# Seven block products in place of eight for the first product of a second mixture of experts

## The chip, the cores and the metric

The kernel runs on one core of one Trainium2 chip. The metric is the device time in microseconds (us) of one execution. Three runs of the kernel before took 2059.77, 2060.48 and 2062.86 us; their median is 2060.48 us. One more execution was profiled.

The engines are named as in the profile: PE is TensorE (matrix products; PEld its weight loads), DVE is VectorE, ACT is ScalarE, POOL is GpSimd, SP is SyncE, which here only issues DMA transfers.

## The reference

Three stages follow one another on 2304 tokens of width 512:

```
x   = attention(q, k, v)        # 4 x 8 heads, 576 positions, windows of 32, plain or dilated by 4
h   = x @ w_in                  # 512 -> 2048        (first mixture, rational activation)
x   = (P(h) / Q(h)) @ w_out     # 2048 -> 512, P and Q polynomials of third and second degree
Pr  = exp(x @ w_gate - max); 8 times: divide by row sums, by column sums, times N / 8
out = sum over e of Pr[:, e] * (relu(x @ w1[e]) @ w2[e])     # 8 experts, 512 -> 1024 -> 512
```

Inputs and outputs are float32. The products of the two mixtures are made of pieces: each operand is scaled by a power of two and split into a high and a low part in float16 (in the first mixture's second product, without scaling, in a reduced float32), and hi*hi + hi*lo + lo*hi are summed, so each product costs three matrix instructions.

## The kernel before, in words

**First mixture.** It runs in 96 steps (`NS1`): six blocks of 384 tokens (`NB`, `TB`) times sixteen blocks of 128 features. A step makes 12 instructions of the first product (`rat_l1`, L574 to L576), the rational function on ACT, DVE and POOL (`rat_a`, `rat_b`, `rat_c`, L589 to L612), and three steps later 12 instructions of the second product (`rat_l2`, L626 to L628). Attention of later batches is woven between the steps. When a block of tokens is done, `x2_evac` takes it out of PSUM, `x2_absmax` finds its scale (L655), and `x2_split` makes the float16 pieces of the block on ACT and DVE (L151, L154), which stay in SBUF.

**Second mixture.** It runs in 288 slots (`NS2`): eight experts, nine pairs of token tiles of 128 (`PAIRS`), four groups of hidden features (`NP`), each with 128 features of the lower and 128 of the upper half. In a slot `moe_l1` makes the first product directly: 2 halves x 4 blocks of the contraction x 3 instructions = 24 instructions of 256 columns (L826). `moe_a` applies the relu on ACT (L843), forms four sums and differences of blocks on POOL (L845), and splits seven blocks into hi and lo on ACT and DVE (L848, L849). Two slots later (`LAG2`) `moe_l2` makes the second product as seven block products instead of eight (`PRODS`): 21 instructions of 256 columns (L867 to L869). After the fourth group `y_evac` puts the seven products together on DVE (L905) and adds the gated result to a sum in SBUF (L913), which is written out once, during the last expert (L915).

**Weights.** For each expert, eight pieces of 512 KB (`raw_load`, on SP's queue) are loaded twice: once to find the scale (`raw_absmax`, L759), once to be split (`raw_part`, L786 on ACT and L789 on DVE). Pieces of `w2` also get four differences on POOL (`raw_diff`, L796). Times of this work are written out by hand with `at(...)`; what is pinned by `pin` stays behind the same engine's work on the current group. Within that, a scheduler of the framework fixes the order of each engine's instructions when the program is built, and each engine then runs its own list in that order.

**PSUM.** Two sets of four banks: `bank` for products that are taken out at once, `long` for sums that live over many instructions. The second product of the second mixture uses all four `long` banks.

## Time and profile before

| what | value |
|---|---|
| median of three runs | 2060.48 us |
| span of the profiled execution | 2059.4 us |
| PE busy | 1975.8 us, 96% of the span |
| DVE, ACT, POOL busy | 1360.0, 1033.1, 876.1 us |
| chain that ended last | PE 70%, DVE 8%; L826 35%, L867 to L869 10% each |
| moved by DMA | 112.32 MB |

The profiled execution took 2059.4 us from its first to its last instruction; that is 1.1 us less than the median of the runs. Busy time is the union of an engine's instructions. Matrix instructions overlap in the records, so their pitch (start to start) tells more than their duration. A group of the page names the source line, engine, operation and tiles, the count, the busy time, the mean of one, and the idle time before them with what ended it.

### The profile page before, as it was taken

To read this page: it belongs to the slowest core of one execution; us is meant where nothing else is said; L and a number is where in the kernel's file an instruction comes from. 1 tells how busy PE (TensorE), PEld (TensorE's weight loads), DVE (VectorE), ACT (ScalarE), POOL (GpSimd) and SP (SyncE) were. 2 spreads that over 40 slices of the span, in tenths; PEclk is the share of its full clock that TensorE was granted. 3 is DMA by queue.
4 is the path that set the end of the run, shared out by engine and by line. 5 is a ranking of instruction groups with operands and counts; after the bars stand their busy time and mean duration, and the time that the engine had idled before them with its cause. 6 is when DMAs were issued, how large, how long until landed. Compare 5 with 4: busy or idle time off the path is not lost.

```text
span 2059.4 us, 42175 instructions
## 1 busy us (share of the span) xinstructions
PE 1975.8 (96%) x16764; PEld 1707.6 (83%) x16764; DVE 1360.0 (66%) x2441; ACT 1033.1 (50%) x1981; POOL 876.1 (43%) x1471
## 2 busy tenths in 40 slices
PE   7588999999999999999999999999999999999998
PEld 6466767776778888888888888888888888888887
DVE  5898899889997654655665564565556546556344
ACT  5777888776775344344434434433443443334332
POOL 1232233222244355445545545454454545446333
PEclk7789999999999999999999999999999999999999
DMA  6642220113111111300211130021112102110000
GB/s 169 165 139 77 61 73 13 35 28 98 32 32 52 52 42 32 93 22 22 78 52 37 35 90 27 27 83 42 32 42 83 32 22 88 37 32 12 32 32 32
DMA packets 171637, 112.32 MB, mean 55 GB/s; under 512 B 74160, under 2 KB 156080, under 8 KB 171440
## 3 DMA queue, kind: packets, MB, share of 16 engines
q1 hardware_dynamic: 171440, 109.64, 18.3%
q8 instruction: 131, 2.15, 0.4%
q14 instruction: 66, 0.54, 0.1%
HBM read 104.88 MB, written 4.72 MB: 53 GB/s over the span
## 4 chain that ended last, share of the span: by engine, by line
PE 70%; DVE 8%; ACT 2%; POOL 1%; issue 1%; DMA 1%; SPq 0%; DVEq 0%; POOLq 0%; ACTq 0%
PE h2ps L826 35%; PE yps L867 10%; PE yps L868 10%; PE yps L869 10%; POOL ht L845 1%; DVE slab_a L603 1%; DVE slab_q L592 1%; DVE slab_q L602 1%; DVE slab_t L604 1%; PE o1ps L626 1%; DVE slab_t L594 1%; PE o1ps L627 1%; PE o1ps L628 1%; DMA wraw<-in_moe_w_dram 1%; DVE slab_t L593 1%
## 5 line engine op out<-in xcount | busy, mean ns | idle before, releaser
L845 POOL TENSOR_TENSOR ht<-ht 128x128 f32<-128x128 f32 x1152 | 607.9, 548 | 719.4 <-ACT ht L843 697.1
L826 PE MATMUL h2ps<-xs,w1t 128*128 128x256 f16 x6912 | 803.8, 273 | 0.0
L826 PEld LDWEIGHTS <-w1t 128*128 128x128 f16 x6912 | 675.6, 98 | 78.9 <-issue 1.1
L849 DVE TENSOR_TENSOR hs<-ht,hs 128x896 f16<-128x896 f32 x288 | 331.8, 1153 | 557.1 <-ACT hs L848 557.1
L848 ACT ACTIVATE hs<-ht 128x896 f16<-128x896 f32 x288 | 273.2, 950 | 623.7 <-POOL ht L845 623.6
L867 PE MATMUL yps<-w2t,hs 128*128 128x256 f16 x2016 | 548.1, 273 | 0.3 <-DVE ys L905 0.3
L868 PE MATMUL yps<-w2t,hs 128*128 128x256 f16 x2016 | 548.1, 273 | 0.0
L869 PE MATMUL yps<-w2t,hs 128*128 128x256 f16 x2016 | 545.6, 273 | 0.0
L843 ACT ACTIVATE ht<-h2ps 128x512 f32<-128x512 f32 x288 | 170.2, 592 | 213.9 <-PE h2ps L826 212.1
L868 PEld LDWEIGHTS <-hs 128*128 128x128 f16 x2016 | 197.2, 98 | 23.8 <-issue 0.5
L869 PEld LDWEIGHTS <-hs 128*128 128x128 f16 x2016 | 197.3, 98 | 23.0
L867 PEld LDWEIGHTS <-hs 128*128 128x128 f16 x2016 | 197.3, 98 | 22.6
L612 POOL TENSOR_TENSOR slab_g<-slab_t,slab_g 128x384 fp32r<-128x384 f32 x96 | 107.0, 1117 | 240.7 <-ACT slab_g L611 176.4
L905 DVE TENSOR_TENSOR ys<-yps,ys 128x256 f32<-128x256 f32 x468 | 168.3, 418 | 53.0 <-ACT ys L900 45.1
L627 PE MATMUL o1ps<-slab_g,wo_hi 128*128 128x384 f32 x384 | 139.7, 364 | 2.4 <-POOL slab_g L612 2.1
L628 PE MATMUL o1ps<-slab_g,wo_lo 128*128 128x384 f32 x384 | 132.6, 345 | 0.0
L626 PE MATMUL o1ps<-slab_g,wo_hi 128*128 128x384 f32 x384 | 105.0, 374 | 9.6 <-ACT slab_g L611 8.7
L574 PE MATMUL h1ps<-x,wi 128*128 128x384 f16 x256 | 85.7, 335 | 9.9 <-DMA qks<-in_q_dram 3.5
L913 DVE SCALAR_TENSOR_TENSOR acc<-ys,pwt,acc 128x512 f32<-128x512 f32 x112 | 90.8, 811 | 0.0
L575 PE MATMUL h1ps<-x,wi 128*128 128x384 f16 x256 | 85.3, 333 | 0.0
L576 PE MATMUL h1ps<-x,wi 128*128 128x384 f16 x256 | 85.1, 332 | 0.0
L626 PEld LDWEIGHTS o1ps<-slab_g,wo_hi 128*128 128x128 f32 x384 | 68.6, 194 | 17.0 <-ACT slab_g L611 12.5
(163 smaller groups left out, 2456.1 us busy)
## 6 DMA issues: line engine op xcount, KB each, us to landing
wraw<-in_moe_w_dram SPq DMA_DIRECT2D x192, 256.0 KB
wraw<-in_moe_w_dram SPq DMA_DIRECT2D x128, 128.0 KB
wst<-in_moe_w_in_dram SPq DMA_DIRECT2D x16, 512.0 KB
xs<-in_v_dram SPq DMA_DIRECT2D x6, 768.0 KB
xs<-in_moe_w_out_dram SPq DMA_DIRECT2D x9, 512.0 KB
out_dram<-acc SPq DMA_DIRECT2D x16, 256.0 KB
wost<-in_moe_w_out_dram SPq DMA_DIRECT2D x7, 512.0 KB
...
```

Of the source, the lines that this page charges most:

```text
L626: nc.tensor.matmul(ob[dd], hi, d["gh"], start=first, stop=False)
L627: nc.tensor.matmul(ob[dd], hi, d["gl"], start=False, stop=False)
L628: nc.tensor.matmul(ob[dd], lo, d["gh"], start=False, stop=last)
L826: nc.tensor.matmul(o, w[:, wh, half, kk, :], x, start=half == 0 and kk == 0 and wh == 0 and xh == 0, stop=half == 1 and kk == KD - 1 and w ...
L843: nc.scalar.activation(E[:, 0:4, :].rearrange("p n c -> p (n c)"), hp, AF.Relu)
L845: i = nc.gpsimd.tensor_tensor(out=E[:, o, :], in0=E[:, x, :], in1=E[:, y, :], op=op)
L848: behind["a"] = nc.scalar.activation(hh, E[:, 1:8, :], AF.Copy).ins.name
L849: behind["v"] = nc.vector.tensor_tensor(out=hl, in0=E[:, 1:8, :], in1=hh, op=ALU.subtract).ins.name
L867: nc.tensor.matmul(o, hh[:, a - 1, :], w[:, m, 0, :], start=i == 0 and half == 0, stop=False)
L868: nc.tensor.matmul(o, hh[:, a - 1, :], w[:, m, 1, :], start=False, stop=False)
L869: nc.tensor.matmul(o, hl[:, a - 1, :], w[:, m, 0, :], start=False, stop=i == NP - 1 and (half == 1 or b == 3))
L905: nc.vector.tensor_tensor(out=o, in0=s0, in1=s1, op=ALU.add)
```

## The change

The first product of the second mixture becomes a product of 2 x 2 blocks with seven block products. The three groups (`NG3`) have 768 tokens: six tiles, two halves of 384. A piece of work `m` is one expert, one group of tokens and one of the four feature groups; there are 96 of them (`NM`). Each has seven units (`moe_unit`), one per block product, of 6 instructions with 384 columns (L924). Four of the products are summed up in one PSUM bank (`l1a`), whose partial sums ACT copies out between them; three go to a second bank (`l1b`), from which DVE adds them. POOL forms the four differences of the hidden blocks (L946; for the first four pieces DVE does it), and ACT and DVE split seven blocks of 384 columns (L990, L991).

The block sums of the tokens are made once, in `mix_sub` and `mix_put`, and both float16 pieces of seven blocks per group are written to a tensor in HBM (`xd`, L754). `x_load` brings them back on SP's queue, one block of 384 KB at a time, whenever the group of tokens changes, into eight buffers (L910). The weights `w1` get four sums and differences as well (`raw_diff`, L873, on DVE for the first expert and on POOL later), and are split into seven blocks instead of four.

The second product keeps its 21 instructions for each pair of tiles and feature group, but runs 28 units (`LG`) behind the first one, three block products after each unit. Its result is scaled by the gate on ACT (L1043) and written to `out` with a plain transfer for the first expert, and added to `out` in HBM by a DMA with `accum_op` on POOL's queue for the seven others (L1048): 63 transfers of 512 KB. All large buffers become parts of a few rooms (`roomA`, `roomV0`, ...), which is why the tiles have new names below.

```diff
+    def mix_src(G, c):
+        if c in (CT1, CT2):
+            return room("x2f", [P, 2, XQ], F32)[:, c == CT2, :]
+        n, h = {CX00: (0, 0), CX10: (0, 1), CT4: (0, 1), CT3: (1, 0), CX11: (1, 1)}[c]
+        return xhome(2 * G + n)[:, h * XQ:(h + 1) * XQ]
+
+    def mix_sub(G, c):
+        a, b = {CT1: (CT3, CX00), CT2: (CX11, CT1), CT3: (CX11, CT3), CT4: (CX10, CT2)}[c]
+        nc.vector.tensor_tensor(out=mix_src(G, c), in0=mix_src(G, a), in1=mix_src(G, b), op=ALU.subtract)
+
+    def mix_put(G, c, slot):
+        t = room(f"mix{slot}", [P, 2, XQ], F16)
+        src, s = mix_src(G, c), s_x2[:, G:G + 1]
+        split_hi(src, t[:, 0, :], s)
+
+        def low():
+            split_lo(src, t[:, 0, :], t[:, 1, :], s)
+            o = (G * 7 + c) * 2 * XQ
+            nc.sync.dma_start(out=xd[:, o:o + 2 * XQ], in_=t.rearrange("p h x -> p (h x)"))
+
+        mixed[G, c] = t.rearrange("p h (k t) -> p h k t", t=TB)
+        return low
...
+    def raw_diff(e, k, n):
+        w = k // NP
+        o, x, y = DIFFS[w][n]
+        d = room("wd", [P, 4, EH], F32)
+        a, b = ({"b": raw[e, k], "d": d}[z[0]][:, int(z[1]), :] for z in (x, y))
+        eng = nc.gpsimd if e else nc.vector
+        pin("p" if e else "v", eng.tensor_tensor(out=d[:, o, :], in0=a, in1=b, op=ALU.add if w == 0 and n == 0 else ALU.subtract))
...
-        if w == 0:
-            t = w1s[e, i] = sb.tile([P, 2, 2, KD, P], F16, tag=W1_AT[(e * NP + i) % 6], name="w1t")
-            v = t.rearrange("p s h k c -> p s (h k c)")
-            parts = [(src, v[:, 0, :], v[:, 1, :], e1[:, c:c + 1])]
-        else:
-            t = w2s[e, i] = sb.tile([P, 7, 2, EH], F16, tag=W2_AT[(e * NP + i) % 6], name="w2t")
-            b = src.rearrange("p (n x) -> p n x", n=4)
-            d = w4f[:, 1024:2048].rearrange("p (n x) -> p n x", n=4)
-            parts = [(b[:, 1:4, :], t[:, 0:3, 0, :], t[:, 0:3, 1, :], e2[:, c:c + 1]), (d, t[:, 3:7, 0, :], t[:, 3:7, 1, :], e2[:, c:c + 1])]
-
-        def hi(x, h, l, sc):
+        sc = (e1, e2)[w][:, e % 2:e % 2 + 1]
+        src = raw[e, k]
+        t = room(f"w{w + 1}s{(e * NP + i) % 5}", [P, 7, 2, EH], F16)
+        (w1s, w2s)[w][e, i] = t
+        parts = [(src[:, 1:4, :], t[:, 0:3, 0, :], t[:, 0:3, 1, :]), (room("wd", [P, 4, EH], F32), t[:, 3:7, 0, :], t[:, 3:7, 1, :])]
...
+    def x_load(k, c):
+        if k < len(runs):
+            t = xr[k, c] = room(f"xr{(7 * k + c) % 8}", [P, 2, 2, TB], F16)
+            o = (runs[k][1] * 7 + c) * 2 * XQ
+            nc.sync.dma_start(out=t.rearrange("p h k t -> p (h k t)"), in_=xd[:, o:o + 2 * XQ])
+
+    mac = {}
+    PROD1 = ((0, CX00), (2, CT4), (5, CT2), (1, CX10), (3, CT1), (4, CT3), (6, CX11))
+
+    def moe_l1(m, pos, ps, group):
+        start, stop = pos in (0, 3, 5), pos in (1, 3, 6)
+        v, i = divmod(m, NP)
+        e, G = GV[v]
+        wx_, c = PROD1[pos]
+        k = run_of[v]
+        w, x = w1s[e, i], xr[k, c]
+        for kk in range(2):
             for wh, xh in ((0, 0), (0, 1), (1, 0)):
-                o = hp[:, 2 * P * half:2 * P * (half + 1)]
-                if tb == ta + 1:
-                    x = x2[n][:, xh, kk, t * P:(t + 2) * P]
-                else:
-                    o = o.rearrange("p (b c) -> p b c", b=2)
-                    x = xp[:, :, xh, kk, t * P:(t + 1) * P]
-                nc.tensor.matmul(
-                    o,
-                    w[:, wh, half, kk, :],
-                    x,
-                    start=half == 0 and kk == 0 and wh == 0 and xh == 0,
-                    stop=half == 1 and kk == KD - 1 and wh == 1,
+                mm = nc.tensor.matmul(
+                    ps,
+                    w[:, wx_, wh, kk * P:(kk + 1) * P],
+                    x[:, xh, kk, :],
+                    start=start and kk == 0 and wh == 0 and xh == 0,
+                    stop=stop and kk == 1 and wh == 1,
+                    skip_group_check=True,
                 )
-
-    hs = []
-
-    def moe_a(st):
-        hp = cur[NS1 + st]
-        if not hs:
-            t = sb.tile([P, 3, 7, P], F16, tag="IG", name="hs")
-            one_ = [sb.tile([P, 7, P], F16, tag=x, name="hs") for x in ("IQ", "akT", "apT0")]
-            hs.extend((t[:, n], one_[n]) for n in range(3))
-        E = sb.tile([P, 8, P], F32, tag=("IT", "IA")[st % 2], name="ht")
-        nc.scalar.activation(E[:, 0:4, :].rearrange("p n c -> p (n c)"), hp, AF.Relu)
-        for o, x, y, op in ((4, 0, 2, ALU.add), (5, 4, 1, ALU.subtract), (6, 1, 0, ALU.subtract), (7, 3, 5, ALU.subtract)):
-            i = nc.gpsimd.tensor_tensor(out=E[:, o, :], in0=E[:, x, :], in1=E[:, y, :], op=op)
-        behind["p"] = i.ins.name
-        hh, hl = hs[st % 3]
-        behind["a"] = nc.scalar.activation(hh, E[:, 1:8, :], AF.Copy).ins.name
-        behind["v"] = nc.vector.tensor_tensor(out=hl, in0=E[:, 1:8, :], in1=hh, op=ALU.subtract).ins.name
-        cur[NS1 + st] = hh, hl
+                if start and kk == 0 and wh == 0 and xh == 0:
+                    group["first"] = mm.ins.name
+        if stop:
+            after_mm(mm, group["guests"])
+        if i == NP - 1 and v == last_of[k]:
+            if c == CT4:
+                x_load(k + 2, CX00)
+            else:
+                x_load(k + 1, c + 1)
...
+    def combine(m, o, x, y, op):
+        d = mac[m]
+        a, b = (d["E"][:, z, :] if z < 4 else d["D"][:, z - 4, :] for z in (x, y))
+        eng = nc.vector if m < NP else nc.gpsimd
+        i = eng.tensor_tensor(out=d["D"][:, o - 4, :], in0=a, in1=b, op=op)
+        if m >= NP:
+            behind["p"] = i.ins.name
+
+    def moe_unit(u):
+        m, pos = divmod(u, 7)
+        if pos == 1:
+            m -= 1
+        if not 0 <= m < NM:
+            return
+        if pos == 0:
+            mac[m] = dict(
+                A=bank("l1a"), E=room("E03" + "ab"[m % 2], [P, 4, TB], F32), D=room("E47", [P, 4, TB], F32),
+            )
+        d = mac[m]
+        if pos == 3:
+            d["Y"] = bank("l1b")
+        ps = d["Y" if pos in (1, 3, 5) else "A"]
+        if pos in (0, 3, 5):
+            d[pos] = dict(ps=ps, used=0, guests=[])
+        group = d[{0: 0, 2: 0, 4: 0, 6: 0, 3: 3, 5: 5, 1: 5}[pos]]
+        moe_l1(m, pos, ps[:, 0:TB], group)
+        if pos in (0, 5):
+            fresh[:] = [group]
+        ps = ps[:, 0:TB]
+        E = d["E"]
+        if pos in (0, 2, 4):
+            nc.scalar.activation(E[:, (0, 2, 3)[pos // 2], :], ps, AF.Copy)
+        elif pos == 3:
+            nc.vector.tensor_tensor(out=E[:, 0, :], in0=ps, in1=E[:, 0, :], op=ALU.add)
+            nc.scalar.activation(E[:, 0, :], E[:, 0, :], AF.Relu)
+        elif pos == 5:
+            nc.vector.tensor_tensor(out=E[:, 3, :], in0=ps, in1=E[:, 3, :], op=ALU.add)
+        elif pos == 6:
+            nc.scalar.activation(E[:, 1, :], ps, AF.Relu)
+            combine(m, 6, 1, 0, ALU.subtract)
+        else:
+            nc.vector.tensor_tensor(out=E[:, 2, :], in0=ps, in1=E[:, 2, :], op=ALU.add)
+            nc.scalar.activation(E[:, 2:4, :], E[:, 2:4, :], AF.Relu)
+            combine(m, 4, 0, 2, ALU.add)
+            combine(m, 5, 4, 1, ALU.subtract)
+            combine(m, 7, 3, 5, ALU.subtract)
+            h = d["h"] = room(f"hs{m % 6}", [P, 2, 7, TB], F16)
+            for src, o in ((E[:, 1:4, :], slice(0, 3)), (d["D"], slice(3, 7))):
+                behind["a"] = nc.scalar.activation(h[:, 0, o, :], src, AF.Copy).ins.name
+                behind["v"] = nc.vector.tensor_tensor(out=h[:, 1, o, :], in0=src, in1=h[:, 0, o, :], op=ALU.subtract).ins.name
...
+        if gate_ready[0]:
+            y_out(v, p, yd)
+        else:
+            pend.append((v, p, yd))
+
+    def y_out(v, p, yd):
+        e, G = GV[v]
         for n in range(2):
-            if e == 0:
-                if gate_ready[0]:
-                    y_scale(tt[n])
-                else:
-                    pend.append(tt[n])
-                continue
-            nc.vector.scalar_tensor_tensor(out=a[n], in0=d[n], scalar=gate_col(e, tt[n]), in1=a[n], op0=ALU.mult, op1=ALU.add)
-            if e == NE - 1:
-                nc.sync.dma_start(out=out[tt[n] * P:(tt[n] + 1) * P, :], in_=a[n])
-
-    def y_scale(tt):
-        nc.scalar.activation(acc[tt], acc[tt], AF.Copy, scale=gate_col(0, tt))
+            nc.scalar.activation(yd[:, n, :], yd[:, n, :], AF.Copy, scale=gate_col(e, 2 * TPB * G + TPB * n + p))
+        dst = bass.AP(out.tensor, (2 * TPB * G + p) * P * DM, [[DM, P], [TPB * P * DM, 2], [1, DM]])
+        if e == 0:
+            nc.sync.dma_start(out=dst, in_=yd)
+        else:
+            nc.gpsimd.dma_start(out=dst, in_=yd, accum_op=ALU.add)
...
+    side_mode[0] = 1
+    for u in range(NU + LG):
+        if u == LG:
+            side_mode[0] = 2
+        if u == 0:
+            rat_b(NS1 - 1)
+        moe_unit(u)
+        run_slot(US + 2 * u)
+        if u < 2 * LAG:
+            rat_l2(NS1 - LAG + u // 2, u % 2)
+        if u == 1:
+            rat_c(NS1 - 1)
+        for q in range(3 * (u - LG), 3 * (u - LG + 1)):
+            if 0 <= q < NQ:
+                moe_l2(q)
+        run_slot(US + 2 * u + 1)
```

DVE's list near the end of the first mixture, kernel before: L592 to L604 are the rational function, L789 splits the first expert's `w2`.

```order
L675 TENSOR_REDUCE lg<-lgps 128x24
L789 SCALAR_TENSOR_TENSOR w2t<-wraw,sm,w2t 128x3x256
L676 TENSOR_SCALAR lg<-lg,sm 128x24
L592 SCALAR_TENSOR_TENSOR slab_q<-slab_q,cf,slab_a 128x384
L593 TENSOR_TENSOR slab_t<-slab_t,h1ps 128x384
L602 SCALAR_TENSOR_TENSOR slab_q<-slab_q,slab_a 128x384
L594 SCALAR_TENSOR_TENSOR slab_t<-slab_t,cf,h1ps 128x384
L603 SCALAR_TENSOR_TENSOR slab_a<-slab_q,slab_a 128x384
L789 SCALAR_TENSOR_TENSOR w2t<-w_6297,sm,w2t 128x4x256
L604 SCALAR_TENSOR_TENSOR slab_t<-slab_t,sm,slab_a 128x384
L602 SCALAR_TENSOR_TENSOR slab_q<-slab_q,slab_a 128x384
```

The same place in the changed kernel: L663 to L675 are the rational function (L663 was L592, L675 was L604), L887 splits weights, L873 forms their differences.

```order
L663 SCALAR_TENSOR_TENSOR roomA<-roomA,cf 128x384
L664 TENSOR_TENSOR roomA<-roomA,h1ps 128x384
L873 TENSOR_TENSOR roomA<-roomA 128x256 x2
L675 SCALAR_TENSOR_TENSOR roomA<-roomA,sm 128x384
L665 SCALAR_TENSOR_TENSOR roomA<-roomA,cf,h1ps 128x384
L873 TENSOR_TENSOR roomA<-roomA 128x256
L663 SCALAR_TENSOR_TENSOR roomA<-roomA,cf 128x384
L664 TENSOR_TENSOR roomA<-roomA,h1ps 128x384
L673 SCALAR_TENSOR_TENSOR roomA<-roomA 128x384
L873 TENSOR_TENSOR roomA<-roomA 128x256
L665 SCALAR_TENSOR_TENSOR roomA<-roomA,cf,h1ps 128x384
L674 SCALAR_TENSOR_TENSOR roomA<-roomA 128x384
```

Four instructions per piece of weights (L873) have joined DVE's list between those of the rational function; in the kernel before they stood in POOL's.

POOL's list inside an expert, kernel before: L845 forms the hidden blocks' sums and differences of a slot (`ht`), L796 those of a piece of `w2` (`wraw`) in a spare buffer (`w4`).

```order
L845 TENSOR_TENSOR ht_11274<-ht_11274 128x128 x4
L796 TENSOR_TENSOR w4_6297<-wraw_11132 128x256
L796 TENSOR_TENSOR w4_6297<-wraw_11132,w4_6297 128x256
L845 TENSOR_TENSOR ht_11330<-ht_11330 128x128 x4
L796 TENSOR_TENSOR w4_6297<-wraw_11132 128x256
L796 TENSOR_TENSOR w4_6297<-wraw_11132,w4_6297 128x256
L845 TENSOR_TENSOR ht_11396<-ht_11396 128x128 x4
L845 TENSOR_TENSOR ht_11462<-ht_11462 128x128 x4
```

The same in the changed kernel: L946 forms those of the hidden blocks (inputs in `roomA` or `roomV1` for every other piece of work, results in `roomIG`), L873 those of weights, L1048 adds a result to `out`.

```order
L946 TENSOR_TENSOR roomIG_6584<-roomIG_6584,roomA_66 128x384
L946 TENSOR_TENSOR roomIG_6584<-roomA_66,roomIG_6584 128x384
L873 TENSOR_TENSOR roomA_66<-roomA_66 128x256 x4
L946 TENSOR_TENSOR roomIG_6584<-roomV1_6583 128x384
L1048 DMA out_0_dram<-roomV1_6583 128x2x512
L946 TENSOR_TENSOR roomIG_6584<-roomV1_6583 128x384
L946 TENSOR_TENSOR roomIG_6584<-roomIG_6584,roomV1_6583 128x384
L946 TENSOR_TENSOR roomIG_6584<-roomV1_6583,roomIG_6584 128x384
L873 TENSOR_TENSOR roomA_66<-roomA_66 128x256 x4
L946 TENSOR_TENSOR roomIG_6584<-roomA_66 128x384
L1048 DMA out_0_dram<-roomA_66 128x2x512
```

The four instructions of a piece of work are three times as wide and stand apart, and the transfer to `out`, which waits for ACT's scaling, stands between the first and the other three.

## Rows read from the trace of the kernel before

**Rows 1.** The page's busy time by engine, share of the span.

```profile
PE 1975.8 (96%) x16764; PEld 1707.6 (83%) x16764; DVE 1360.0 (66%) x2441; ACT 1033.1 (50%) x1981; POOL 876.1 (43%) x1471
```

**Rows 2.** Windows: stretch, its length, busy us of each engine (instructions), granted clock.

```profile
core 0: us, PE busy (x) PEld busy (x) DVE busy (x) ACT busy (x) POOL busy (x), PEclk, DMA share, GB/s
525.00:629.00 104.00, 99.52 (x604) 76.04 (x603) 101.33 (x169) 77.63 (x156) 40.26 (x37) 1.00 0.06 17
616.00:2053.00 1437.00, 1433.69 (x13094) 1282.76 (x13092) 816.56 (x1275) 575.58 (x777) 697.18 (x1273) 1.00 0.15 45
```

**Rows 3.** Waits of PE from 700 to 2050 us: total, times, longest.

```profile
PE smps L119 <- DVE gs L697: 0.5, 1, 0.5
PE yps L867 <- DVE ys L905: 0.3, 1, 0.3
```

**Rows 4.** Chain in order of time: start us, us, what; two neighbours of many.

```profile
1171.26 2.62 PE h2ps L826 x24
...
1176.17 2.62 PE h2ps L826 x24
```

**Rows 5.** Timeline of PE: first and last of nine at an even pitch.

```profile
459.02 0.33 PE L574 MATMUL h1ps<-xs,wi 128*128 128x384 f16 x1
...
460.32 0.33 PE L576 MATMUL h1ps<-xs,wi 128*128 128x384 f16 x1
```

**Rows 6.** Groups of DVE from 430 to 629 us: busy us, mean ns, idle before.

```profile
L592 DVE SCALAR_TENSOR_TENSOR slab_q<-slab_q,cf,slab_a 128x384 f32<-128x384 f32 x40 | 29.1, 728 | 3.3 <-ACT slab_a L591 3.3
...
L154 DVE SCALAR_TENSOR_TENSOR xs<-x2f,sm,xs 128x384 f16<-128x384 f32 x12 | 7.2, 632 | 0.0
...
L655 DVE TENSOR_REDUCE sm<-x2f 128x1 f32<-128x1536 f32 x3 | 5.2, 1748 | 0.0
...
L789 DVE SCALAR_TENSOR_TENSOR w1t<-wraw,sm,w1t 128x1024 f16<-128x1024 f32 x4 | 5.1, 1279 | 0.8 <-ACT w1t L786 0.8
...
L648 DVE TENSOR_TENSOR x2f<-o1ps,xs 128x384 f32<-128x384 f32 x8 | 4.1, 552 | 1.1 <-PE o1ps L628 1.1
...
L789 DVE SCALAR_TENSOR_TENSOR w2t<-w,sm,w2t 128x1024 f16<-128x1024 f32 x3 | 4.1, 1358 | 0.0
...
L789 DVE SCALAR_TENSOR_TENSOR w2t<-wraw,sm,w2t 128x768 f16<-128x768 f32 x3 | 3.8, 1253 | 0.0
```

**Rows 7.** Timeline of DVE and POOL around 587 us.

```profile
586.60 1.43 DVE L592 SCALAR_TENSOR_TENSOR slab_q<-slab_q,cf,slab_a 128x384 f32<-128x384 f32 x1
...
586.60 1.02 POOL L612 TENSOR_TENSOR slab_g<-slab_t,slab_g 128x384 fp32r<-128x384 f32 x1 [1.04 <-ACT slab_g L611]
...
587.95 0.54 DVE L593 TENSOR_TENSOR slab_t<-slab_t,h1ps 128x384 f32<-128x384 f32 x1
```

**Rows 8.** Groups of the page, second mixture: busy us, mean ns, idle, what ended it.

```profile
L845 POOL TENSOR_TENSOR ht<-ht 128x128 f32<-128x128 f32 x1152 | 607.9, 548 | 719.4 <-ACT ht L843 697.1
...
L849 DVE TENSOR_TENSOR hs<-ht,hs 128x896 f16<-128x896 f32 x288 | 331.8, 1153 | 557.1 <-ACT hs L848 557.1
...
L848 ACT ACTIVATE hs<-ht 128x896 f16<-128x896 f32 x288 | 273.2, 950 | 623.7 <-POOL ht L845 623.6
```

**Rows 9.** Timeline of POOL, two slots of the second mixture.

```profile
1698.54 3.46 POOL L845 TENSOR_TENSOR ht<-ht 128x128 f32<-128x128 f32 x4 [3.55 <-ACT ht L843]
...
2036.90 1.81 POOL L845 TENSOR_TENSOR ht<-ht 128x128 f32<-128x128 f32 x4 [3.09 <-ACT ht L843]
```

**Rows 10.** Chain in order of time: two loads of 512 KB that it waits for.

```profile
467.88 4.17 DMA wraw<-in_moe_w_dram
...
512.25 4.84 DMA wraw<-in_moe_w_dram
```

**Rows 11.** Waits of SP's queue: total, times, longest.

```profile
SPq L753 <- DVE w2t L789: 133.5, 8, 47.7
```

**Rows 12.** Timeline of the end: PE's last, and SP's last issue.

```profile
2052.51 0.38 PE L869 MATMUL yps<-w2t,hs 128*128 128x256 f16 x2
...
2056.25 0.33 SPq L915 DMA_DIRECT2D out_dram<-acc  x1
```

More of the change, by code (lines that the diff above doesn't have):

```diff
@@ L67, with homes @@
     sb = ctx.enter_context(tc.tile_pool(name="sb", bufs=1))
+    hbm = ctx.enter_context(tc.tile_pool(name="hbm", bufs=1, space=bass.MemoryType.DRAM))
+    ZX, ZR, ZE = 37888, 74752, 125952
+    ROOMS = {"A": 132096, "V0": 16384, "V1": 17408, "V2": 32768, "IG": 6144}
+    HOME = {}
+    def homes(base, size, names, where="A", era=0):
+        for name in names.split():
+            HOME[name] = where, era, base, size
+            base += size
+            assert base <= ROOMS[where]
+        return base
@@ new lines, with room @@
+    homes(0, 10752, "hs0 hs1 hs2", "V2", 2)
+    homes(0, 6144, "E47", "IG", 2)
+    homes(7168, 3072, "mix4 mix5", "V0", 2)
+    homes(0, 3072, "mix6 mix7", "V1", 2)
+    rooms = {}
+    def room(tag, shape, dt):
+        where, era, a, size = HOME[tag]
+        n = math.prod(shape[1:]) * (2 if dt == F16 else 4)
+        assert n <= size, (tag, shape)
+        old = rooms.get(where)
+        if old is None or old[0] < era:
+            old = rooms[where] = era, sb.tile([P, ROOMS[where] // 4], F32R if era == 1 else F32, tag=where, name=f"room{where}")
+        assert old[0] == era, (tag, old[0])
+        t = old[1][0:shape[0], a // 4:(a + n) // 4]
+        if dt != (F32R if era == 1 else F32):
+            t = t.bitcast(dt)
+        d = "abcd"[:len(shape) - 1]
+        if len(d) > 1:
+            t = t.rearrange(f"p ({' '.join(d)}) -> p {' '.join(d)}", **dict(zip(d[1:], shape[2:])))
+        return t
@@ L713 @@
     NS1 = NB * NF1
-    acc = {}
     pw = {}
@@ new lines @@
+    runs, run_of, last_of = [], [], {}
+    for vi, (_, G) in enumerate(GV):
+        if not runs or runs[-1][1] != G:
+            runs.append((vi, G))
+        run_of.append(len(runs) - 1)
+        last_of[len(runs) - 1] = vi
+    xr = {}
+    def x_load(k, c):
[3 more added lines that the diff above has]
+            nc.sync.dma_start(out=t.rearrange("p h k t -> p (h k t)"), in_=xd[:, o:o + 2 * XQ])
@@ L888, in gate_col, with y_evac @@
         return pw[e, "pw"][:, tt:tt + 1]
-    ys = []
-    def y_evac(e, j):
-        tt = PAIRS[j][1], PAIRS[j][0]
-        a = [acc_tile(x) for x in tt]
-        if not ys:
-            ys.append(sb.tile([P, 2048], F32, tag="W7", name="ys"))
-        u, v, x, w = (ys[0][:, n * EH:(n + 1) * EH] for n in range(4))
-        d = a if e == 0 else [ys[0][:, 1024 + n * DM:1024 + (n + 1) * DM] for n in range(2)]
+    def y_evac(v, p):
+        yd = room(f"yd{(3 * v + p) % 2}", [P, 2, DM], F32)
+        d = yd[:, 1, :], yd[:, 0, :]
+        vv = room("yv", [P, EH], F32)
@@ new lines, in mix_at, with at_step @@
+    def mix_at(G, when, s0, slot0):
+        for dt, c, slot in zip(s0, (CX00, CX10, CT1, CX11, CT2, CT3, CT4), (0, 1, 2, 3, 0, 1, 2)):
+            if c in (CT1, CT2, CT3, CT4):
+                when(dt, mix_sub, G, c)
+            when(dt, mix_put, G, c, slot0 + slot)
+            if c == CX11:
+                when(dt + (0.5 if G < 2 else 2), x2_logits, G)
+    def at_step(t, fn, *a):
+        at(int(4 * t) + 1, fn, *a)
+    mix_at(0, at_step, (56, 57, 58, 59, 61, 62, 63), 0)
+    mix_at(1, at_step, (69, 70, 71, 72, 74, 75, 76), 0)
@@ L1072 @@
+        at_u(u0 + 59, raw_scale, e, 0)
+        at_u(u0 + 60, raw_scale, e, 1)
+        for i in range(4):
+            prep_at(US + 2 * (u0 + (58.5 + 7 * i if i else 62)), e, i, 1)
+            prep_at(US + 2 * (u0 + LG + (77.5 + 3 * (i - 1) if i else 58)), e, NP + i, 1)
+    use.sort(key=lambda x: x[0])
+    for n, (_, e, kx, first) in enumerate(use):
+        s = 4 * 63 if n < 2 else use[n - 2][0]
+        assert s < first, (n, e, kx, s, first)
         at(s, raw_load, e, kx)
```

379 lines of the change are left out of this document (179 added, 200 removed).

## The prediction

> **What bounds the kernel now.** I read the busy times first: PE is busy for 96% of the span, far ahead of DVE [rows 1]. That is an average, so I went to windows next. The reader should see two stretches there. From 616 us on, which is the second mixture, PE is busy for 1433.7 of 1437.0 us at the full granted clock (1.00, the 2.4 GHz level), while DVE, ACT and POOL are busy for 57, 40 and 49% [rows 2]. The waits agree: PE waited for other engines less than 1 us between 700 and 2050 us [rows 3]. So in this stretch, 70% of the time, only fewer or shorter matrix instructions help, and each us of them is a us of the span as long as nobody else is late. The last 24 steps of the first mixture, 525 to 629 us, are another matter: DVE is busy for 101.3 of 104.0 us [rows 2]. PE's own need there is 24 steps of 24 instructions with 384 columns, 576 x 0.1625 = 94 us at the pitch found below. DVE sets the end, and work added to DVE there lengthens the span.
>
> **First product, the term that is saved.** The chain of waits shows slots 4.91 us apart, with 24 first-product instructions in 2.62 us of each [rows 4], so one of 256 columns takes 0.1092 us. The 6912 of them cost 754.6 us. The change needs 8 experts x 3 groups x 4 features x 7 products x 6 = 4032 instructions of 384 columns. Float16 instructions of that size ran in the first mixture at 9 starts in 1.30 us [rows 5], 0.1625 us each: 655.2 us. That is -99.4 us. The second product keeps its 6048 instructions and its 2.29 us per slot. A unit of the new loop is then 6 x 0.1625 + 9 x 0.1092 = 1.96 us of PE.
>
> **DVE at the end of the first mixture: +18 us.** Prices are from [rows 6]; an element costs (1279 - 632) / 640 = 1.01 ns more, so 768 elements split in 1.02 us and subtract in 0.94 us (552 ns for 384), and 256 subtract in 0.42 us. Token blocks: 5 x 4 splits of 0.63 us go (12.6 us), two groups x (7 x 1.02 + 4 x 0.94) = 21.8 us come, +9.2. `w1` of the first expert: 4 x (1.02 + 1.28 + 4 x 0.42) for 4 x 1.28, +10.8. `w2`: 3 x 4 differences come over from POOL, +5.0. Three fewer scale computations of seven tiny instructions, -3; starts that overlap by 0.08 us [rows 7], -1. Sum +21. Against this, POOL loses those twelve instructions, and DVE is blocked by POOL: an instruction of 0.61 us took 1.43 us because POOL started one of 1.02 us at the same moment [rows 7], and the mean of its kind is 728 ns [rows 6]. I take back 3 us: +18. If PE's own need hides half of it the term is 8; if every new instruction is slowed as the old ones are (728/614), it is 25.
>
> **The start of the second mixture: +6 us (0 to 15).** For 28 units no second product runs, so PE needs 0.98 us per unit, 6.8 us per piece of work. DVE's share of a piece, with the differences that it makes for the first four, is 7 x 0.55 + splits of 1152 and 1536 columns, from 1153 ns for 896 [rows 8] plus 1.01 ns per element 1.41 and 1.80 us: 7.1 us. It also has the rest of the first mixture and part of the third group's block sums. In the changed order I count some 43 us of DVE work, priced so, between the end of the first mixture and the fourth hidden piece, and 41 us of PE work up to the first product that needs it. Slowed by a seventh, DVE is 6 us behind.
>
> **Later second products: +12 us (0 to 60).** PE meets the fourth piece of each pass tightly: its last product ends in the unit before six others, and its difference blocks are read after 0.98 + 5 x 1.96 + 0.98 + 0.33 = 12.1 us of PE work. The way there is DVE's add 0.55, ACT's relu on 768 columns 0.82 (950 ns for 896 [rows 8]), three POOL instructions of 1.02 [rows 7], ACT's split 1.63, DVE's split 1.80, five handovers for which I allow 0.1 each, and once DVE's 1.41 us in front of POOL: 9.8 us. The other 2.3 us must hold whatever stands ahead in three queues. That POOL's time varies is plain: the same four instructions took 1.81 and 3.46 us in two slots [rows 9], and its idle time shows it had room for that [rows 8]. In the 23 passes after the first I take half a us each. All other hidden pieces have more than 20 us. DVE's load stays under PE: of an expert's 84 x 1.96 = 165 us it needs 12 x 4.9 for hidden pieces, 9 x 7 x 0.42 for the results and 8 x (2.3 + 1.2) for weights (1.2 from L655 by size [rows 6]), 113 us or 68%.
>
> The Trainium skill, "SBUF — State Buffer" (section "SBUF: two separate sides"), says that VectorE with two SBUF inputs and GpSimd share a port pair, and that whoever starts second is blocked for the whole instruction. The timeline bears it out: 1.43 us is 0.41 more than POOL's 1.02 [rows 7]. By this rule the way takes 9.8 us, as above. If the two only shared the port, it would take 8.4 us and the 12 us would be near nothing, a total of 1989 us; the rows speak for the rule.
>
> **End and small terms: +4 us.** Between PE's last instruction (2052.89) and the end (2059.4) lie 6.5 us [rows 12]. ACT's two scalings replace DVE's two sums. The last transfer is 512 KB that must be read, added and written instead of 256 KB; loads of 512 KB took 4.2 to 4.8 us [rows 10], against 3.2 us from the last issue now. An issue on POOL is not in the trace; 0.3 us (SP's record [rows 12]) to 1.0 us (a POOL instruction [rows 7]) bound it, unless the last rival holds. Together +3, from 0 to 6. Twelve more small gate products, under 0.1 us each, add 1 us.
>
> **Sum.** -99.4 + 18 + 6 + 12 + 3 + 1 = -59.4. The profiled execution spans 2059.4 us, 1.1 us below the median of the runs: 2000.0 + 1.1, so 2001 us.
>
> **Rivals.** *All new work hides* (0.18). The waits of PE were under 1 us with three engines half idle [rows 2, 3]. With +8 on DVE, nothing at the start or later, and +4 at the end, 1973 us. Against it speaks DVE's 97% before 629 us.
>
> *The hidden pieces come late* (0.18). If queueing takes 2.5 us more than the 2.3 us of room in each of 23 passes, the term is 58 instead of 12: 2047 us. For it: POOL and DVE work that excludes each other grows. Against it: only one piece in four is tight.
>
> *x comes late* (0.04). A new block must land within 8 units, 15.7 us, and stands in SP's queue behind loads of weights; one of these waited 16.7 us on average and 47.7 at most [rows 11]. With 16 changes of group and 3 us each, 2049 us. Such waits occur where the load is early, so I give it little.
>
> *Slower: POOL holds the hidden pieces* (0.09). In 21 passes a transfer to `out` can stand in POOL's queue before the three sums, as the changed order shows, and wait for ACT, which waits for DVE. If the queue stands still for as long as a transfer takes, 4.8 us [rows 10], it costs 21 x 4.8 = 101 us more: 2102 us. It decides from 2.8 us per pass (59 / 21) upward. For it: POOL's list is fixed. Against it: an issue only writes what the transfer needs.
>
> The Trainium skill warns of this in "SBUF — State Buffer", in the section named above: such an issue writes its descriptors through the port that DVE can block. No run here shows it yet.
>
> **How the numbers follow.** The forecast has 0.51, with its own range from 1982 to 2024. The range from 1971 to 2050 takes in the first three rivals' times and leaves out little more than the slower one. A difference of 0.2%, 4 us, is what a measurement can tell. Faster: 0.51 + 0.18 + 0.17 + 0.03 = 0.89; the same 0.02; slower 0.09.
>
> **What would show it.** In the changed profile: L924 at a pitch of 0.1625 us and the second product at 0.109; the first L924 some 18 us after 616 us, where the first L826 stood, with DVE over 95% busy before; waits of PE for DVE or ACT at L1013 and L1014 near 12 us in total, none at L924 for a DMA; POOL's transfers short in its queue. Wrong would be a second mixture whose PE stands idle for more than 40 us, or transfers on POOL that last for microseconds.

## The result, and the profile after

The changed kernel is slower: 2083.7 us in the median of four runs (2079.94 to 2087.59), beside 2061.62 us for the kernel before in the same set. The ratio is 1.0104, with a 95% interval from 1.0087 to 1.0121. The forecast was 2001.0 us with a range up to 2050, so it missed by 83 us and on the wrong side. The profiled execution is the slowest of the four, 2087.59 us with a span of 2085.8, 3.9 us above the median.

Busy times of the page, as in [rows 1]. PE fell from 96% to 92%; DVE, ACT and POOL rose.

```profile
PE 1914.8 (92%) x13914; PEld 1433.3 (69%) x13914; DVE 1515.0 (73%) x2572; ACT 1229.1 (59%) x2328; POOL 944.9 (45%) x846
```

The windows answer to [rows 2]: busy us (instructions) of PE, weight loads, DVE, ACT and POOL, then granted clock, DMA share and GB/s.

```profile
525.00:629.00 104.00, 94.95 (x593) 71.15 (x592) 103.64 (x182) 79.18 (x152) 27.97 (x22) 1.00 0.18 54
616.00:660.00 44.00, 42.31 (x241) 31.35 (x242) 39.20 (x62) 29.43 (x62) 11.43 (x10) 1.00 0.03 10
660.00:700.00 40.00, 29.69 (x205) 17.37 (x202) 36.95 (x64) 28.04 (x38) 0.00 (x0) 0.85 0.48 152
700.00:800.00 100.00, 94.06 (x701) 70.28 (x702) 72.78 (x157) 42.20 (x63) 35.95 (x29) 0.94 0.31 99
800.00:2000.00 1200.00, 1142.35 (x8612) 841.96 (x8611) 784.57 (x1094) 653.56 (x949) 706.64 (x605) 1.00 0.42 104
2000.00:2086.00 86.00, 73.96 (x603) 58.53 (x600) 36.73 (x62) 31.48 (x48) 27.26 (x22) 0.97 0.25 38
```

Before, PE idled 3.3 us in the whole second mixture. Now it idles 57.65 us between 800 and 2000 us alone, while DVE, ACT and POOL are busy for 65, 54 and 59%: none of them is full, and PE still waits. Between 660 and 700 us it idles a quarter of the time, DVE is at 92%, and the clock granted averages 0.85, so part of the stretch ran at the 1.2 GHz level.

PE's waits from 700 to 2050 us answer to [rows 3]: total us, times, longest.

```profile
PE l1a L924 <- ACT roomA L973: 18.0, 20, 2.3
PE l1a L924 <- ACT roomV L973: 15.6, 23, 2.0
PE l1b L924 <- DVE roomV L978: 6.9, 8, 0.9
PE yps L1013 <- DVE roomA L1034: 6.0, 12, 0.9
PE yps L1013 <- DVE roomV L1034: 4.2, 7, 0.9
PE smps L173 <- DVE gs L792: 4.0, 1, 4.0
PE l1b L924 <- DMA roomA<-xd: 3.0, 1, 3.0
PE yps L1013 <- ACT roomA L884: 2.7, 5, 0.6
PE yps L1015 <- DVE roomV L991: 2.1, 5, 0.4
PE yps L1013 <- ACT roomV L884: 1.0, 2, 0.5
```

A wait is counted from the end of the record before it. That record lasts 0.33 or 0.27 us where the next instruction could have come after 0.162 or 0.109, so by estimate each place costs some 0.17 us more than is listed, and the loss counted further down is greater than the sum of the list.

The greatest wait, 33.6 us in 43 places (18.0 and 15.6 in the list), is not in the second product, where the prediction looked. It is in the first. Four of the seven block products of a piece add up in one bank (`l1a`), and between them ACT copies the partial sum out (L973). PE cannot go on in that bank before the copy is done. One place in full, as the timelines show it. PE:

```profile
1103.62 1.14 PE L924 MATMUL l1a<-roomA 128*128 128x384 f16 x6 [0.55 <-ACT roomA L973]
...
1109.37 1.78 PE L924 MATMUL l1a<-roomA 128*128 128x384 f16 x10 [0.91 <-ACT roomA L973]
```

ACT:

```profile
1104.52 0.51 ACT L976 ACTIVATE roomA<-roomA 128x384 f32<-128x384 f32 x1
1107.45 1.48 ACT L990 ACTIVATE roomV<-roomIG 128x1536 f16<-128x1536 f32 x1 [2.42 <-POOL roomIG L946]
1108.84 0.47 ACT L973 ACTIVATE roomA<-l1a 128x384 f32<-128x384 f32 x1
```

POOL, and DVE beside it:

```profile
1104.34 1.00 POOL L946 TENSOR_TENSOR roomIG<-roomIG,roomV 128x384 f32<-128x384 f32 x1
1105.43 1.99 POOL L946 TENSOR_TENSOR roomIG<-roomV,roomIG 128x384 f32<-128x384 f32 x1
```

```profile
1104.65 1.91 DVE L991 TENSOR_TENSOR roomV<-roomV,roomV 128x1152 f16<-128x1152 f32 x1 [1.88 <-ACT roomV L990]
```

PE's six products in the bank end at 1104.76, and the copy could run from then. It runs at 1108.84, and PE's next products there stand 0.91 us for it. Ahead of the copy in ACT's queue is a split (L990) that stood 2.42 us for POOL's third combine (L946). That combine took 1.99 us where the one before it took 1.00, with DVE's split (L991) of the same piece running beside it. The copy needed nothing of this; it only came later in the list. In 19 of the 43 places (15.1 of the 33.6 us) the run of ACT's work that ends in the late copy begins with such a split. In 12 more (12.9 us) it begins with a relu (L984) that waits for DVE's add L983. That add stood in 6 of them (7.5 us) behind a maximum (L850) that waited for a load of weights, in 5 (4.4 us) behind a split (L991) that waited for ACT, and in one behind a split of weights. In 6 (3.7 us) it begins with L884, which waits for POOL's differences of weights.

What matched: the pitch of the first product, first in the span, and the end.

```profile
635.67 0.33 PE L924 MATMUL l1a<-roomA 128*128 128x384 f16 x1
...
657.95 2.11 PE L924 MATMUL l1a<-roomA 128*128 128x384 f16 x12
...
2075.73 0.27 PE L1015 MATMUL yps<-roomA 128*128 128x256 f16 x1
```

Twelve products in 2.11 us are (2.11 - 0.33) / 11 = 0.162 us each. From PE's last instruction to the end it is 2085.8 - 2076.0 = 9.8 us, 3.3 more than in [rows 12].

### The profile page after: what moved, and what is told of

It is laid out like the page before. It is cut to its first block, busy times and chain, and to the rows that moved or that the text cites. A ratio compares the mean times of both kernels' runs of the same rounds, so it can differ in the third digit from the quotient of the medians.

```text
span 2085.8 us, 36459 instructions
## 1 busy us (share of the span) xinstructions
PE 1914.8 (92%) x13914; PEld 1433.3 (69%) x13914; DVE 1515.0 (73%) x2572; ACT 1229.1 (59%) x2328; POOL 944.9 (45%) x846
## 5 line engine op out<-in xcount | busy, mean ns | idle before, releaser
L924 PEld LDWEIGHTS <-roomA 128*128 128x128 f16 x3276 | 320.9, 98 | 223.1 <-issue 59.2
L924 PE MATMUL l1a<-roomA 128*128 128x384 f16 x1872 | 358.3, 327 | 28.5 <-ACT roomA L973 16.8
L924 PE MATMUL l1b<-roomA 128*128 128x384 f16 x1404 | 274.4, 330 | 14.5 <-DVE roomV L978 5.3
L946 POOL TENSOR_TENSOR roomIG<-roomV 128x384 f32<-128x384 f32 x92 | 112.8, 1227 | 262.6 <-ACT roomV L980 112.8
L873 POOL TENSOR_TENSOR roomA<-roomA 128x256 f32<-128x256 f32 x224 | 211.2, 962 | 22.3 <-DVE roomA L887 8.4
L946 POOL TENSOR_TENSOR roomIG<-roomA 128x384 f32<-128x384 f32 x92 | 110.4, 1200 | 195.2 <-ACT roomA L980 99.4
L1013 PE MATMUL yps<-roomA 128*128 128x256 f16 x630 | 170.9, 273 | 7.0 <-ACT roomA L884 2.7
L1013 PE MATMUL yps<-roomA,roomV 128*128 128x256 f16 x630 | 171.6, 275 | 2.4 <-DVE roomA L1034 1.5
L1014 PE MATMUL yps<-roomA,roomV 128*128 128x256 f16 x630 | 172.1, 275 | 0.0
L1015 PE MATMUL yps<-roomA 128*128 128x256 f16 x630 | 170.6, 274 | 1.0 <-DVE roomA L991 1.0
L1015 PE MATMUL yps<-roomA,roomV 128*128 128x256 f16 x630 | 170.3, 275 | 1.3 <-DVE roomV L991 1.3
L1014 PE MATMUL yps<-roomA 128*128 128x256 f16 x630 | 171.4, 273 | 0.0
L645 PE MATMUL h1ps<-roomA 128*128 128x384 f16 x384 | 130.6, 341 | 16.4 <-DVE roomA L665 8.2
L991 DVE TENSOR_TENSOR roomV<-roomIG,roomV 128x1536 f16<-128x1536 f32 x48 | 87.6, 1825 | 79.2 <-ACT roomV L990 79.2
L887 DVE SCALAR_TENSOR_TENSOR roomA<-roomA,sm 128x768 f16<-128x768 f32 (+1 forms) x92 | 123.8, 1355 | 28.3 <-ACT roomA L884 27.6
L991 DVE TENSOR_TENSOR roomA<-roomIG,roomA 128x1536 f16<-128x1536 f32 x48 | 94.2, 1962 | 68.0 <-ACT roomA L990 68.0
L698 PE MATMUL o1ps<-roomIG,roomV 128*128 128x384 f32 x384 | 137.6, 358 | 4.2 <-POOL roomIG L683 4.1
L884 ACT ACTIVATE roomA<-roomA,sm 128x768 f16<-128x768 f32 (+1 forms) x92 | 94.5, 1037 | 79.7 <-POOL roomA L873 50.7
L699 PE MATMUL o1ps<-roomIG,roomV 128*128 128x384 f32 x384 | 131.3, 342 | 0.0
L646 PE MATMUL h1ps<-roomA 128*128 128x384 f16 x384 | 130.0, 339 | 0.0
L647 PE MATMUL h1ps<-roomA 128*128 128x384 f16 x384 | 129.7, 338 | 0.0
```

The lines of the kernel that those rows point to most:

```text
L645: mm = nc.tensor.matmul(hp, whi, xb[:, 0, kk, :], start=kk == 0, stop=False)
L646: nc.tensor.matmul(hp, whi, xb[:, 1, kk, :], start=False, stop=False)
L647: nc.tensor.matmul(hp, wlo, xb[:, 0, kk, :], start=False, stop=kk == KD - 1)
L698: nc.tensor.matmul(ob[dd], hi, d["gl"], start=False, stop=False)
L699: nc.tensor.matmul(ob[dd], lo, d["gh"], start=False, stop=last)
L873: pin("p" if e else "v", eng.tensor_tensor(out=d[:, o, :], in0=a, in1=b, op=ALU.add if w == 0 and n == 0 else ALU.subtract))
```

## The experiments

All are edits of the changed kernel, and each set was timed beside the kernel before. The count of matrix instructions between 800 and 1950 us says how much PE got done in the steady part. The run e4, in which PE never waits there, did 8814; a kernel with n lost (1 - n/8814) x 1150 us. The count is of the profiled execution, which in e7 was 7 us faster than the median and in e14 5 us slower. Medians are not of one chip, so the ratios to before are the safer figures; the kernel before took 2060.9 to 2061.7 us beside them.

| run | median us | ratio to before (95%) | n | lost us |
|---|---|---|---|---|
| changed kernel | 2083.7 | 1.0087 to 1.0121 | 8233 | 75.8 |
| e1 combines on DVE | 2028.71 | 0.9835 to 0.9865 | 8624 | 24.8 |
| e2 no transfers on POOL | 2057.93 | 0.9973 to 0.9996 | 8427 | 50.5 |
| e3 differences on DVE | 2053.22 | 0.9946 to 0.9974 | 8505 | 40.3 |
| e4 no weights prepared | 2001.6 | 0.9702 to 0.9731 | 8814 | 0 |
| e7 split after third copy | 2034.69 | 0.9842 to 0.9893 | 8651 | 21.3 |
| e8 no maxima | 2028.94 | 0.9823 to 0.9867 | 8632 | 23.7 |
| e13 split after second copy | 2075.34 | 1.0056 to 1.0083 | 8326 | 63.7 |
| e14 other split later | 2054.98 | 0.9955 to 0.9983 | 8464 | 45.7 |
| e9 = e7 + e1 | 2015.02 | 0.9763 to 0.979 | 8792 | 2.9 |

**What crowds the three queues.** e1 changes one line of `combine`, and the two lines below it that keep POOL's work on weights behind the combines go too:

```diff
-        eng = nc.vector if m < NP else nc.gpsimd
+        eng = nc.vector
```

> All three combine instructions of a piece (L946) on VectorE instead of GpSimd; nothing else edited. Theory A (TensorE waits at the first product's bank because ScalarE's copy L973 stands behind L990, which waits for GpSimd's three combines in series): of the changed kernel's 2083.7 us, 40 to 50 go, to 2035 to 2045, and between 800 and 2000 us the waits of L924 for L973 fall from 33.6 us below 15. Rival B (GpSimd's transfers L1048 hold its queue): 2075 to 2085, the waits stay. Rival C (preparing the next expert's weights stalls VectorE's queue): 2080 to 2100, since VectorE gets 240 x 0.47 = 113 us more.

Measured: 2028.71 us, 55 us less, and PE's waits for the copy fall to 14.6 us. Theory A was right in direction and too modest in size. C's price was too low: between 800 and 2000 us DVE got 344 of these instructions at 0.63 us each, 217 us in place of 113, and the kernel was faster all the same.

e2 stores every output tile by SP:

```diff
-        if e == 0:
-            nc.sync.dma_start(out=dst, in_=yd)
-        else:
-            nc.gpsimd.dma_start(out=dst, in_=yd, accum_op=ALU.add)
+        nc.sync.dma_start(out=dst, in_=yd)
```

> Every scaled output tile is stored by SyncE without the addition in HBM, so that the sum over the experts is left out; GpSimd issues no transfer. Theory A: 2065 to 2078 (the 1.2 us of issue and its wait for L1043 leave GpSimd's queue, the combines stay). Rival B: below 2050. Rival C: 2080 to 2085.

Measured: 2057.93 us, 26 us less, between A's and B's figures. POOL's issue is short, but it is a place in the queue: the group of the changed kernel, 800 to 2000 us (busy us, mean ns, idle before, what ended it), is

```profile
L1048 POOL DMA_DIRECT2D out_dram<-roomV x29 | 34.9, 1204 | 67.1 <-ACT roomV L1043 63.4 <-DVE roomA L991 3.5
```

so 1.2 us of issue, and POOL stood 63 us for ACT's scaling before these 29 issues, and 62 us before the 28 others, with combines listed behind.

e3 changes the same choice in `raw_diff`: `eng = nc.vector` for all experts.

> The 16 differences per piece of raw weights (L873) on VectorE for every expert instead of GpSimd. Theory A: 2060 to 2075, since the combines stand behind fewer instructions but are still three in series at 1 to 2 us. Rival B: 2080 to 2085. Rival C: 2060 or above 2090, as the stall moves from the wait of L884 for L873 to VectorE's own queue.

Measured: 2053.22 us, 30 us less, better than A's figure and beyond C's.

e4 sets `w1s[e, i], w2s[e, i] = w1s[0, i], w2s[0, i]` and schedules none of the preparation for e > 0.

> Experts 1 to 7 use expert 0's prepared weights, so that loads, maxima, differences and splits of the other seven experts' weights are left out. Theory A: 2055 to 2070 (GpSimd's queue loses 218 instructions of 0.96 us, the combines remain). Rival B: 2075 to 2085. Rival C: below 2040, the waits of L924 for L973 nearly gone.

Measured: 2001.6 us, 82 us less. C's figure was met, although C's reason can't be the whole of it, since e1 gains 55 us with all preparation in place. The window says that PE never idles:

```profile
800.00:1950.00 1150.00, 1150.00 (x8814) 862.17 (x8812) 604.47 (x867) 572.76 (x861) 489.04 (x395) 1.00 0.30 63
```

The same places in the run's POOL groups say something more. The combine (now L953) is no faster, 1995 ns for the third of a piece:

```profile
L953 POOL TENSOR_TENSOR roomIG<-roomV,roomIG 128x384 f32<-128x384 f32 x42 | 83.8, 1995 | 3.3
```

A slow combine costs PE nothing as long as little else stands in the queues.

e8 leaves out `raw_absmax` for experts 1 to 7.

> The maxima of the raw weights (L850) of experts 1 to 7, with the eight loads per expert that they alone need, are left out; the scales of expert 0 are used. Rival C in the form that VectorE's queue stops at L850 for a load: 2055 to 2065. Theory A: 2068 to 2080, as GpSimd's differences, combines and transfers are all still there.

Measured: 2028.94 us, 55 us less, below the figures of both. The maxima cost DVE 56.6 us of busy time in 1200 and stopped its queue for loads for 27.7 us more; e8 takes both away, and the loads with them, so it does not tell them apart. Savings of e1, e2, e3 and e8 add up to 166 us, twice what there was to gain: each works on the same waits.

**Whether the order alone does it.** e7 moves no work. It puts the split of the combined pieces later, with a dependency on a copy:

```diff
-            for src, o in ((E[:, 1:4, :], slice(0, 3)), (d["D"], slice(3, 7))):
+            split(E[:, 1:4, :], slice(0, 3))
+            held.append(lambda dep: split(d["D"], slice(3, 7), dep))
...
+            if pos == 4 and held:
+                held.pop()(cp.ins.name)
```

> No work is moved to another engine: the split of the four combined pieces (L990 on ScalarE, L991 on VectorE) is only put later in the queues, behind the next piece's third copy of the first product's bank. Theory A (the copy stands behind L990, which waits for GpSimd): 2055 to 2070 where the changed kernel took 2083.7, and hardly any wait of L924 for the copy begins with L990 waiting for GpSimd. Rival C (the weights' preparation alone): 2078 to 2086. Rival D (the single buffer of the combined pieces then binds): over 2090.

Measured: 2034.69 us, 49 us less, more than A expected. PE's waits are now (800 to 1950 us; by e7's line numbers the copy is L975, and L984 is the relu that empties the bank, L980 in the changed kernel):

```profile
PE yps L1027 <- ACT roomA L884: 3.3, 8, 0.5
PE l1a L924 <- ACT roomV L975: 2.9, 6, 0.5
PE l1a L924 <- ACT roomA L984: 2.2, 5, 0.9
...
PE l1a L924 <- ACT roomA L975: 1.1, 5, 0.2
```

None of the late copies stands behind the split any more. But the scheduler rewrites the lists of all engines at any edit: by the traces, some 300 of ACT's 2328 instructions in e7 no longer stand in the old sequence, and some 150 in e2, which does not touch ACT's work. So two more runs were made. e13 has `pos == 2` for `pos == 4`, e14 holds back the other split instead.

> As e7, but the split of the combined pieces is put behind the next piece's second copy instead of its third, two units earlier. Theory A with the distance counting: GpSimd has some 4 us less time before the split stands at the head of ScalarE's queue, so part of e7's gain goes, 2045 to 2070. Rival E (any change of the lists in the queues gives the gain, whatever is put later): 2028 to 2042, as e7's 2034.7.

> A control: as e7, but the split that does not wait for GpSimd (of the other three pieces) is put behind the third copy, and the one that waits for GpSimd stays where it was. Theory A: little or nothing gained, 2065 to 2095. Rival E: 2028 to 2050.

e13: 2075.34 us, above A's range; some 210 of ACT's instructions stand in another place, and 8 us go. PE's greatest waits (800 to 1950 us):

```profile
PE l1a L924 <- ACT roomV L975: 15.5, 19, 1.3
PE yps L1027 <- ACT roomA L884: 13.2, 5, 2.9
PE l1a L924 <- ACT roomA L984: 6.4, 7, 1.3
PE yps L1027 <- ACT roomV L884: 5.2, 2, 2.6
```

In 13 of the 19 late copies (13.0 us) ACT's work still begins with the split that stands for POOL, and they are all third copies of a piece, as are the 19 (15.1 us) of the changed kernel; in e7, where the split stands behind the third copy, there is none. So a list that is merely rewritten does not give the gain. But the loss stayed for another reason too: the second products now wait 18.4 us for weights that ACT splits late (L884), 3.2 us in the changed kernel. How much of the difference between e13 and e7 is the distance is not shown.

e14: 2054.98 us, 29 us less, which neither theory had. Its POOL group shows why (800 to 1950 us, first the changed kernel, then e14):

```profile
L946 POOL TENSOR_TENSOR roomIG<-roomV,roomIG 128x384 f32<-128x384 f32 x39 | 70.7, 1814 | 3.1
```

```profile
L946 POOL TENSOR_TENSOR roomIG<-roomV,roomIG 128x384 f32<-128x384 f32 x40 | 46.0, 1149 | 3.1
```

With DVE's first split of a piece put later, POOL's third combine takes 1.15 us instead of 1.81 (1.13 instead of 1.51 in the pieces whose input lies in `roomA`). So the control was none: it took 0.4 to 0.7 us that DVE adds out of the same chain, and ACT's half of that split, some 1.15 us, out of the way of the copy as well. The two are not told apart. The waits for the copy fell from 33.6 to 2.8 us, and PE waited for the relu that empties the bank instead:

```profile
PE l1a L924 <- ACT roomA L984: 21.7, 7, 3.1
PE yps L1027 <- ACT roomA L884: 3.3, 9, 0.5
PE l1a L924 <- ACT roomA L975: 2.8, 6, 0.5
```

**The start of the second mixture.** e5 puts the first four pieces' combines on POOL, e6 keeps one of eight gate steps.

> The combines of the first four pieces on GpSimd too, which VectorE does in the changed kernel; this moves only the start of the second mixture. If VectorE's load binds there (12 x 0.47 = 5.6 us less on it): the first second product comes 4 to 8 us earlier than 703.4 and the time is 2075 to 2080. If the chain of gate steps binds: no difference, 2081 to 2086.

> One of the gate's eight normalization steps is kept, seven are left out. If the gate's steps (small products in TensorE's queue that wait for VectorE, 4.0 us at 702.9) bind the start of the second mixture: first second product at 692 to 698, 2070 to 2078. If VectorE's other work binds: 700 to 703, 2078 to 2084.

Measured: 2085.01 and 2071.18 us. The combines on DVE are not what binds there; without seven of the gate's steps it is 12.5 us less, some 4 of them in the steady part (the count is 8263). The first second product came at 706.7 and 699.1 us (703.4 in the changed kernel).

A part of the rest is the clock. In the changed kernel PE stood 1.72 us for DVE before 691.33 us, 3.18 us before 696.58 and 4.02 us, at a step of the gate, before 702.90. From 691.27 to 708.34 the granted clock was 0.50, the 1.2 GHz level, and the first 24 second products ran at that level:

```profile
691.27:708.34 17.07, 9.82 (x40) 6.19 (x40) 12.64 (x32) 3.31 (x6) 0.00 (x0) 0.50 0.00 0
```

```profile
707.57 0.42 PE L1013 MATMUL yps<-roomA,roomV 128*128 128x256 f16 x1
707.79 0.42 PE L1014 MATMUL yps<-roomA,roomV 128*128 128x256 f16 x1
...
708.39 0.27 PE L1013 MATMUL yps<-roomA,roomV 128*128 128x256 f16 x1
708.50 0.27 PE L1014 MATMUL yps<-roomA,roomV 128*128 128x256 f16 x1
```

Their pitch is 0.21 us there, and 0.11 after it: by estimate 24 x 0.10 = 2.5 us. In e6 the clock between 660 and 720 us was 0.97 (second line) in place of 0.83:

```profile
660.00:720.00 60.00, 46.79 (x328) 30.70 (x326) 49.48 (x109) 31.12 (x44) 1.80 (x2) 0.83 0.32 102
660.00:720.00 60.00, 53.53 (x411) 36.76 (x410) 50.48 (x86) 35.96 (x53) 5.05 (x5) 0.97 0.40 128
```

**Put together.** These build on e7.

> The later place of the split (as in the run e7) and the combines on VectorE (as in e1) together. Theory A (both edits take away the same wait, ScalarE's copy behind a split that waits for the combine): 2018 to 2030, little below the better of the two alone (2028.7 and 2034.7). If the two took away different waits, their gains of 55 and 49 us would add up: 1980 to 1995.

> As e7, and the second products follow the first ones at a distance of 26 units instead of 28 (LG). If the length of the stretch with first products alone sets the loss at the start of the second mixture: 3 to 5 us below e7's 2034.7, 2029 to 2032. If the gate's steps set it: no difference, 2032 to 2038.

> As e7, and the gate's eight normalization steps stand at units 36 to 49.5 instead of 23 to 49, so that they come after second products have begun. If these steps, in a stretch with first products alone, cost the 12 us that went when seven of them were left out (e6): 2022 to 2028, first second product at 690 to 697 us. If VectorE's total load there binds: 2032 to 2038.

> The four edits of e1, e7, e10 and e11 together: 2005 to 2020 if the start's loss and the copy's wait are separate; 2020 to 2030 if VectorE's load, with the combines on it, takes the start's gain back.

e9: 2015.02 us, 3 us below A's range and far from a sum of gains. It is the shortest edit with the full result that beats the kernel before by more than 2% (2.2%; e1 alone by 1.5%), and in its steady part PE is all but full:

```profile
800.00:1950.00 1150.00, 1148.10 (x8792) 860.58 (x8791) 908.83 (x1443) 672.19 (x964) 259.16 (x270) 1.00 0.44 109
```

e10: 2039.51 us (0.9881 to 0.991 of before), 5 us above e7 where 4 better was expected, though the two intervals overlap; the first second product came at 701.4 us, no earlier, and PE waited 4.9 us for one load of x. e11: 2031.32 us (0.9843 to 0.987), in between. Its second products begin 12 us earlier than e7's (685.7 against 697.7), but most of that is given back at once, with the granted clock at 0.96 there, as the windows of e7 and e11 show:

```profile
640.00:720.00 80.00, 64.40 (x451) 44.00 (x451) 66.22 (x131) 40.74 (x66) 7.35 (x7) 0.94 0.24 78
720.00:800.00 80.00, 77.27 (x594) 57.65 (x593) 63.67 (x117) 44.59 (x64) 39.48 (x34) 1.00 0.42 139
```

```profile
640.00:720.00 80.00, 73.82 (x551) 52.60 (x551) 71.88 (x135) 45.83 (x73) 8.71 (x9) 1.00 0.28 90
720.00:800.00 80.00, 70.26 (x505) 49.90 (x503) 59.87 (x118) 40.17 (x57) 37.38 (x31) 0.96 0.38 121
```

e12: 2011.74 us (0.9749 to 0.9775), in its better range, and not clearly apart from e9.

## Why the prediction was wrong

- *First product, -99.4 us*: right. The pitch is 0.162 us. (That e4, where PE does not wait, takes 2001.6 us, so near the forecast, is chance: it has none of the 12 us below and more at the start.)
- *End of the first mixture, +18*: right. The first L924 comes at 635.67 us, the first L826 came at 616.80: 18.9, with DVE busy for 103.64 of 104 us.
- *End, +3*: right, 3.3.
- *Start of the second mixture, +6 (0 to 15)*: too small. e4 has no steady loss, so not the 12 us below, and still spans 1999.6, where the forecast had 2000.0 with them: some 12 us more, about 18. By its own figures, 43 x 8/7 - 41, the term would have been 8. What I left out are the gate's steps; in them small products stand in PE's queue for DVE (4.0 us at L173), and e6 finds some 8 of its 12.5 us there. I also priced PE at the full clock there; it was granted 0.83 on average between 660 and 720 us, and 0.86 in e4. What else binds there stays open: e5, e10 and e11 moved single causes and gained little.
- *Later second products, +12 (0 to 60)*: the step that failed. The steady part lost 75.8 us in 1150. The term was made of one wait, of second products for the pieces' difference blocks, which DVE's split (L991) brings last; that wait is 2.1 us in the list. The second product waits 16 us in all, near the 12, but by chance: 10.2 us are for DVE to empty the banks of the last result (L1034), and 3.7 for weights that ACT splits (L884). The largest part is a wait that the prediction did not have, 33.6 us for ACT's copy and 6.9 for DVE's add (L978), which empty the banks of the first product. It worked out the one way with a tight distance, from the fourth piece to its second product, and took every other piece to have 20 us of room. It never asked when banks `l1a` and `l1b` are free for the next product, and so put ACT's copy, half a us long, at no wait at all. The copy runs when everything listed before it on ACT has run, and that includes splits that wait for POOL, whose combines are listed behind differences of weights and issues that wait for ACT. e7 shows it: 49 us go with the order alone.
- *DVE under PE's load, 68%*: right and beside the point. DVE was busy for 757 of 1150 us.
- *Rival "all new work hides", 1973*: wrong where it said that half-idle engines mean no waits. e9 removes the steady waits with DVE at 79%.
- *Rivals "the hidden pieces come late", 2047, and "x comes late", 2049*: not borne out. PE waits 2.1 us for the former (L1015 for L991) and 3.0 us in one place for the latter.
- *Rival "POOL holds the hidden pieces", 2102, for transfers that last 2.8 us or more in the queue*: near in time by chance. An issue lasts 1.2 us, not 4.8, but it stands in line, and e2 finds 26 us. This was one of four things that fed the wait, and it was not the hidden pieces that came late.

The gains of the runs follow the steady loss: e1 55 us for 51 us less lost, e2 26 for 25, e3 30 for 36, e4 82 for 76, e7 49 for 54, e8 55 for 52, e9 69 for 73, e13 8 for 12, e14 29 for 30. So what these edits gain, they gain in the steady part, to some 6 us.

Shown is that the place of the split in ACT's list and the work in POOL's list each move the loss. That DVE's split, by slowing POOL's combine, moves it too is argued from e14, which moved ACT's half of the split as well; in e4 combines of 1995 ns cost nothing. How the loss divides can't be said: these act on one chain, and their gains don't add.
